# Weight conversion with the sign made by the scaling pass, and another order of the opening

## The chip, the core and the metric

One core of a Trainium2 chip runs the whole program. The metric is the device time of one execution in microseconds: the median of several runs. One execution was also recorded by the hardware profiler; its trace is what the rows below come from.

## What is computed

The inputs q, k and v have 8 batches of 8 heads, 576 positions and 64 columns. The weights are float64 in DRAM, since the random numbers are divided by a float64 square root.

```python
# linear attention: softmax of q over its columns, of k over the positions
kv = einsum('bhsd,bhse->bhde', softmax(k, axis=2), v)
x = einsum('bhsd,bhde->bhse', softmax(q, axis=-1), kv)   # then 4608 x 512
# gated layer, 512 -> 1536 -> 512
g = x @ w_gate;  x = (g * sigmoid(g) * (x @ w_val)) @ w_out
# second layer, 512 -> 1024 -> 512
h = x @ w_in2
solu = h * softmax(h, axis=-1)
out = (solu - mean(solu)) / sqrt(var(solu) + 1e-6) * g_ln @ w_out2
```

## The kernel before

**Blocks.** The 4608 tokens go in nine blocks of 512. For every block the kernel makes the attention's rows x, then for each of 12 slices of 128 columns a gate (wg), a value (wv) and their part of the output (y). The gate's products are followed by a Silu on ScalarE (L979), the value's by a product on VectorE (L984), a cast on ScalarE (L989) and a difference on VectorE (L991). All products of the gated layer keep float32 precision by splitting each operand into an upper part (in the rounded type fp32r) and a rest, and by three matmuls (L945 to L947): upper by upper, upper by rest, rest by upper. The second layer comes after all blocks.

**Weights.** A class Weight (L175) holds one tile of 128 x 1024 float64 words, 1 MB. There are 12 tiles wgv0 to wgv11 (a slice of w_gate and of w_val in each, two DMAs of 512 KB) and six tiles wo0 to wo5 of w_out in the opening, and eight tiles w2r0 to w2r7 of the second layer, one in each later block. A float64 word becomes float32 by moving bits: `scale` (L196) reads the upper 32 bits as a float32 and multiplies them by 2^-112, which moves the exponent to its place; `low_bits` (L204) takes the upper bits of the lower word, by reading one byte of it; and `join` (L227) shifts the upper word left by three and ors the lower one in (L236). The shift drops the sign bit, so it is put into the lower word first: either on VectorE in `join` (L232), or on ScalarE in `sign` (L217 to L225), for the nine tiles in the list SIGNED (L1090). Then `upper` casts to fp32r on ScalarE (L247) and `rest` takes the difference on VectorE (L257).

**Order.** Up to the last block every engine gets its instructions in the order in which the program gives them; nothing reorders them later. The opening (L1074) has named tasks, cut into steps at each yield, and the list ORDER (L27) says which task takes its next step. The names: `lk` loads two heads of keys, `lq` half of the queries, `lv` four heads of values, `lw` and `lo` a weight tile; `kT` turns keys, takes their maximum and exponential; `kB` turns them back; `qm`, `qe`, `qn` are maximum, exponential and normalisation of queries; `pk` multiplies keys with values; `pt` turns queries; `px` makes a quarter of x; `cw` and `co` convert a weight tile in four steps (start on ScalarE, join on VectorE, upper on ScalarE, rest on VectorE); `g`, `v`, `o` are gate, value and output of a slice, with g0, v0, g1 and v1 cut into halves that need two quarters of x each. `s` stores a converted tile to DRAM (store, L269) and `b7`, `b8`, `n2` read tiles 7, 8 and 2 back (L276), since only some stay on the chip; a read-back needs a place that another tile has left, by its products and by its store. `*n` puts n small matmuls on constants on TensorE (keep_warm, L1025 to L1029), to keep it at work; 18 of them lead. `t`, `x`, `m`, `a`, `e`, `kv`, `qm`, `qe`, `qn`, `kvl`, `ql1`, `kvn`, `qnx` prepare the attention of the next block and load for it. All DMAs are issued on SP's queue, one after the other; one that waits holds back those behind it. A later block takes its steps from BLOCK_ORDER (L41).

Of the kernel before, what the change touches and what calls it, by code (L numbers as in the profile page):

```python
# [8 lines left out]
F32 = mybir.dt.float32  # L9
# [3 lines left out]
AF = mybir.ActivationFunctionType  # L13
ALU = mybir.AluOpType
# [4 lines left out]
P = 128  # L19
ENGINES = 'PE', 'DVE', 'Activation', 'Pool'  # L20
U8 = mybir.dt.uint8
F16 = mybir.dt.float16
U16 = mybir.dt.uint16
I16 = mybir.dt.int16
COMPUTE = {getattr(mybir.EngineType, x) for x in ENGINES}

ORDER = """  # L27
lw1 lk01 cw1 *14 kT1 lk00 kT0 kT1 lq0 kT1 kT0 *4 kB11 kB10 kT0 kB11 kB00 kB10 qm0 lk10 kB01 cw1 kB00 kT2 lk11 lq1
kB01 qm0 lw0 kT3 kT2 qm1 cw1 qe0 kT2 kT3 kT3 cw0 qn0 *14 kB31 lv0 qm1 kB21 lo0 kB20 qn0 pt1 kB31 pt0 qe1 cw1 lv1
kB30 qn1 kB21 *6 pk1 kB20 pt0 pt1 kB30 pk1 pk1 pk0 pk0 pk0 *5 px1 qn1 lw3 px0 co0 px1 pt2 lw2 pt2 pt3 cw0 co0 pk2  # L30
px0 pk3 pt3 lw4 cw0 pk2 kvl0 pk2 pk3 *11 px2 co0 pk3 px2 lo1 cw3 px0 cw0 px1 px2 *4 px3 lw5 co0 g0 v0 px3 g1 px3 cw2
g0 v0 g0 cw3 cw2 v0 cw2 v1 lw6 g1 cw2 v0 cw3 v0 g1 v1 cw3 g2 v1 o0 cw4 v1 m0 g2 v1 v2 cw4 co1 a0 cw4 co1 ql1 g3 cw5
v2 co1 v2 g3 cw4 o1 cw6 a0 v3 v2 g4 cw5 v3 v3 lw7 cw5 g4 co1 o2 qm cw6 lo2 cw7 v4 v3 co2 qm cw5 e0 cw6 v4 o3 lo3 co2
g5 v4 co2 v5 qe cw6 lw9 v4 g5 co3 g6 co2 cw7 v5 lw10 o4 s2 lw8 qn s3 co3 v5 v5 kv0 v6 kvl1 g6 cw7 cw7 cw8 kv0 kv0 o5
v6 cw8 kv0 v6 co3 v6 g7 lo4 co3 cw8 cw9 v7 g7 cw8 qn cw9 cw10 v7 o6 g8 t1 v7 cw9 m1 v8 t1 v7 cw9 cw10 a1 o7 co4 g8
g9 v8 v8 t1 lw11 co4 cw10 t0 s7 s8 t0 v9 t0 g9 v8 co4 cw11 x1 x0 v9 s9 v9 cw10 x0 co4 t3 x1 t3 a1 g10 s4 x0 t3 x1 o8
t2 lo5 v9 e1 kv1 g10 o9 cw11 kv1 t2 cw11 t2 kv1 kv1 kvn v10 qnx cw11 x2 b7 s10 x3 v10 co5 v10 s1 s0 g11 x2 v10 x3
co5 s11 co5 x3 x2 co5 g11 v11 b8 n2 v11 v11 v11 o10
""".split()

BLOCK_ORDER = """  # L41
# [50 lines left out]
def attention_glu_solu_kernel(  # L92
# [23 lines left out]
    nc = tc.nc  # L116
# [22 lines left out]
    def f32(ap):  # L139
        return ap.bitcast(F32)  # L140

    const = ctx.enter_context(tc.tile_pool(name="const", bufs=1))
# [9 lines left out]
    nc.gpsimd.memset(neg_half, -0.5)  # L152
    floor_bias = const.tile([P, 1], F32, name="floor_bias")
    nc.gpsimd.memset(floor_bias, -15.5 / 32)
    sign_bias = const.tile([P, 1], F32, name="sign_bias")
    nc.gpsimd.memset(sign_bias, 127.5 * 2.0 ** -10)
    warm = const.tile([P, 1], F32, name="warm")
    nc.scalar.activation(out=warm, in_=floor_bias, func=AF.Exp)
    kv_parts = {}
# [15 lines left out]
    class Weight:  # L175
# [6 lines left out]

        def __init__(self, pool, tag, srcs, name, scales=None):
            self.pool, self.tag, self.name, self.scales = pool, tag, name, scales
            self.w, self.done, self.signed = None, False, False
            self.raw = pool.tile([P, 2 * DM, 2], U32, tag=tag, name=f"{name}r")
            n = 2 // len(srcs)
            for i, src in enumerate(srcs):
                nc.sync.dma_start(
                    out=self.raw[:, i * n * DM:(i + 1) * n * DM, :]  # L190
                    .rearrange("p n w -> p (n w)")
                    .rearrange("p (a m) -> p a m", a=src.shape[1]),
                    in_=src,
                )

        def scale(self, on_pool=False):  # L196

            high = f32(self.raw[:, :, 1])
            if on_pool:
                nc.gpsimd.tensor_scalar(out=high, in0=high, scalar1=2.0 ** -112, scalar2=None, op0=ALU.mult)  # L200
            else:
                nc.scalar.activation(out=high, in_=high, func=AF.Copy, scale=2.0 ** -112)

        def low_bits(self):  # L204

# [8 lines left out]
            self.scale()  # L214
            self.low_bits()

        def sign(self):  # L217

            raw = self.raw.rearrange("p n w -> p (n w)")
            top = raw.bitcast(U8).rearrange("p (n b) -> p n b", b=8)  # L220
            sign = raw.bitcast(I16).rearrange("p (n b) -> p n b", b=4)
            nc.scalar.activation(
                out=sign[:, :, 1], in_=top[:, :, 7], func=AF.Prelu, scale=-2.0 ** -10, bias=sign_bias, alpha=2.0 ** 27
            )
            self.signed = True  # L225

        def join(self, pool, tag, bufs=1):  # L227

            low, high = self.raw[:, :, 0], self.raw[:, :, 1]
            if not self.signed:  # L230
                words = self.raw.rearrange("p n w -> p (n w)").bitcast(U16).rearrange("p (n b) -> p n b", b=4)
                nc.vector.tensor_scalar(  # L232
                    out=words[:, :, 1], in0=words[:, :, 3], scalar1=1 << 15, scalar2=None, op0=ALU.bitwise_and
                )
            t = pool.tile([P, 2 * DM], U32, tag=tag, bufs=bufs, name="t")
            nc.vector.scalar_tensor_tensor(  # L236
                out=t, in0=high, scalar=3, in1=low,
                op0=ALU.logical_shift_left, op1=ALU.bitwise_or,
            )
            self.x = f32(t)  # L240
# [833 lines left out]
    def opening():  # L1074
# [12 lines left out]
        }  # L1087
        pools = dict(a=wpool, b=w_b, x=ph1x)
        temps = [(tmp, "t2"), (tmp, "yt")]
        SIGNED = [('wgv', 1), ('wgv', 2), ('wgv', 5), ('wgv', 6), ('wgv', 9), ('wgv', 10), ('wo', 1), ('wo', 3), ('wo', 5)]  # L1090
        joined = []

        def convert(nm, i):
            w, _ = W[("wg", i) if nm == "wgv" else ("wo", 2 * i)]
            w.start()
            if (nm, i) in SIGNED:
                w.sign()
            yield
            w.join(*temps[len(joined) % 2])
            joined.append(i)  # L1100
            yield
            w.upper()
            yield
            w.rest()
# [72 lines left out]
        for i in range(NF):  # L1177
            add(f"lw{i}", load_w1, pools[homes["wgv", i][0]], homes["wgv", i], "wgv", i)
            add(f"cw{i}", convert, "wgv", i)
            add(f"g{i}", gate, i)  # L1180
            add(f"v{i}", value, i)
            add(f"o{i}", emit_o, 0, i, i == 0, False)
        for i in range(NF // 2):
            add(f"lo{i}", load_w1, pools[homes["wo", i][0]], homes["wo", i], "wo", i)
            add(f"co{i}", convert, "wo", i)
# [126 lines left out]

    late = []
    opening()
    pend.clear()
    for j in range(1, NB - 1):
# [379 lines left out]
    a, b = 2 * last, 2 * last + 1  # L1696
# [43 lines left out]
```

## Time and profile before

| | us |
|---|---|
| median of 3 runs | 1341.49 (1341.44 to 1341.50) |
| the profiled execution | 1340.76 |
| its span, first to last instruction | 1339.0 |
| TensorE busy (PE) | 1326.7, 99% |
| VectorE busy (DVE) | 909.5, 68% |
| ScalarE busy (ACT) | 773.9, 58% |
| GpSimd busy (POOL) | 45.2, 3% |

The engines run beside one another, so the busy times don't add up to the span. A matmul's row shows its latency, and matmuls overlap. The share of the clock is the part of full speed (2.4 GHz) that TensorE was granted. Times in rows count from the start of the span.

### The profile page before, as it was taken

The page shows a single profiled execution, that of the slowest core. Times are in us where ns is not written, and L with a number is a line of the kernel's source. Part 1 is how long each engine was busy: PE and PEld are TensorE (multiplying, and loading weights), DVE is VectorE, ACT ScalarE, POOL GpSimd, SP SyncE. Part 2 cuts the span into 40 slices and gives each one's busy share as a digit, 9 for nine tenths or more (in the row PEclk, how much of TensorE's full clock was granted, in tenths as well). Part 3 has the DMA queues.
Part 4 walks back from the last instruction along what each step waited for, and adds up shares of the span by engine and source line. Part 5 has one row for each costly group of instructions (what it writes and reads, how often), then busy time and mean ns, then how long its engine had stood idle before and what let it go on. Part 6 is the DMA issues. An engine that isn't in the chain of part 4 may idle for free.

```text
span 1339.0 us, 17601 instructions
## 1 busy us (share of the span) xinstructions
PE 1326.7 (99%) x6572; PEld 1095.2 (82%) x6572; DVE 909.5 (68%) x1564; ACT 773.9 (58%) x1109; POOL 45.2 (3%) x172
## 2 busy tenths in 40 slices
PE   8999999999999999999999999999999999999999
PEld 6788788888888888888888888888888888888887
DVE  6898675675675685676675573564288778778774
ACT  7998465455455465465465443442276766766764
POOL 2001100000000000000000000000000000000000
PEclk9999999999999999999999999999999999999999
DMA  9965983573574565465557445374377666676651
GB/s 282 286 226 203 361 208 108 187 230 115 178 229 137 173 219 152 157 208 164 172 197 213 160 173 166 145 262 162 118 193 190 173 188 179 165 202 172 163 142 40
DMA packets 242918, 247.58 MB, mean 185 GB/s; under 512 B 152080, under 2 KB 216592, under 8 KB 231824
## 3 DMA queue, kind: packets, MB, share of 16 engines
q1 hardware_dynamic: 242832, 246.45, 60.8%
q8 instruction: 52, 0.85, 0.3%
q14 instruction: 34, 0.28, 0.1%
HBM read 162.01 MB, written 59.24 MB: 165 GB/s over the span
## 4 chain that ended last, share of the span: by engine, by line
PE 90%; ACT 5%; DVE 2%; issue 1%; DMA 1%; SPq 0%; ACTq 0%; DVEq 0%
PE wg L945 7%; PE y L945 7%; PE y L947 7%; PE wv L945 7%; PE y L946 7%; PE wg L947 7%; PE wg L946 7%; PE wv L947 7%; PE wv L946 7%; PE y L1571 5%; PE y L1569 5%; PE y L1570 5%; PE h L945 4%; PE h L947 4%; PE h L946 4%
## 5 line engine op out<-in xcount | busy, mean ns | idle before, releaser
L984 DVE TENSOR_TENSOR st<-st,wv 128x512 f32<-128x512 f32 x108 | 74.1, 686 | 165.4 <-PE wv L947 153.1
L945 PE MATMUL wg<-xh,wgv 128*128 128x512 f32 x432 | 170.0, 394 | 2.3 <-DMA wgv<-w_dram 2.3
L945 PE MATMUL wv<-xh,wgv 128*128 128x512 f32 x432 | 169.3, 392 | 0.2 <-DVE st L984 0.2
L947 PE MATMUL wg<-xh,wgv 128*128 128x512 f32 x432 | 168.5, 390 | 0.0
L946 PE MATMUL y<-a,wo 128*128 128x512 f32 x432 | 168.2, 389 | 0.2 <-DVE a L991 0.2
L947 PE MATMUL y<-a,wo 128*128 128x512 f32 x432 | 168.2, 389 | 0.1
L946 PE MATMUL wg<-xl,wgv 128*128 128x512 f32 x432 | 168.3, 390 | 0.0
L945 PE MATMUL y<-a,wo 128*128 128x512 f32 x432 | 168.3, 390 | 0.0
L946 PE MATMUL wv<-xl,wgv 128*128 128x512 f32 x432 | 168.2, 389 | 0.0
L947 PE MATMUL wv<-xh,wgv 128*128 128x512 f32 x432 | 168.1, 389 | 0.0
L979 ACT ACTIVATE st<-wg 128x512 f32<-128x512 f32 x108 | 64.7, 599 | 141.7 <-PE wg L947 140.9
L991 DVE TENSOR_TENSOR a<-st,a 128x512 fp32r<-128x512 f32 x108 | 74.4, 688 | 76.2 <-ACT a L989 75.5
L1569 PE MATMUL y<-w,zhl 128*128 128x512 f32 (+1 forms) x296 | 113.6, 384 | 0.0
L1570 PE MATMUL y<-w,zhl 128*128 128x512 f32 (+1 forms) x296 | 113.5, 383 | 0.0
L1571 PE MATMUL y<-w,zhl 128*128 128x512 f32 (+1 forms) x296 | 113.5, 383 | 0.0
L989 ACT CAST a<-st 128x512 fp32r<-128x512 f32 x108 | 67.0, 621 | 73.0 <-DVE st L984 46.6
L945 PEld LDWEIGHTS wg<-xh,wgv 128*128 128x128 f32 x432 | 81.1, 188 | 19.3 <-ACT kt L545 2.7
L947 PEld LDWEIGHTS wg<-xh,wgv 128*128 128x128 f32 x432 | 81.1, 188 | 17.8 <-DVE wgv L257 0.7
L947 PEld LDWEIGHTS y<-a,wo 128*128 128x128 f32 x432 | 81.1, 188 | 17.4 <-DVE wo L257 0.6
L946 PEld LDWEIGHTS y<-a,wo 128*128 128x128 f32 x432 | 81.1, 188 | 17.4 <-DVE a L991 0.5
L945 PEld LDWEIGHTS wv<-xh,wgv 128*128 128x128 f32 x432 | 81.1, 188 | 17.3 <-DVE st L984 0.4
L947 PEld LDWEIGHTS wv<-xh,wgv 128*128 128x128 f32 x432 | 81.1, 188 | 17.1
(289 smaller groups left out, 2542.5 us busy)
## 6 DMA issues: line engine op xcount, KB each, us to landing
wgv<-w_dram SPq DMA_DIRECT2D x64, 1024.0 KB, 6.0
yf_dram<-yf SPq DMA_DIRECT2D x56, 512.0 KB, 3.8
yh<-yf_dram SPq DMA_DIRECT2D x18, 896.0 KB, 5.0
yl<-yf_dram SPq DMA_DIRECT2D x18, 896.0 KB, 7.1
w_dram<-wgv SPq DMA_DIRECT2D x10, 1024.0 KB, 11.0
out_dram<-ot SPq DMA_DIRECT2D x35, 256.0 KB, 2.9
kt<-in_k_dram SPq DMA_DIRECT2D x14, 512.0 KB, 4.6
vt<-in_v_dram SPq DMA_DIRECT2D x56, 128.0 KB, 3.4
```

The lines of the kernel that those rows point to most:

```text
L945: nc.tensor.matmul(out=po, lhsT=wh, rhs=rh, start=start, stop=False, **k)
L946: nc.tensor.matmul(out=po, lhsT=wh, rhs=rl, start=False, stop=False, **k)
L947: nc.tensor.matmul(out=po, lhsT=wl, rhs=rh, start=False, stop=stop, **k)
L979: nc.scalar.activation(out=st, in_=pg, func=AF.Silu)
L984: nc.vector.tensor_tensor(out=st, in0=st, in1=pv, op=ALU.mult)
L989: nc.scalar.copy(out=ah, in_=st)
L991: nc.vector.tensor_tensor(out=al, in0=st, in1=f32(ah), op=ALU.subtract)
L1569: nc.tensor.matmul(out=po[:, s], lhsT=zh[:, c, :], rhs=wh[:, s], start=first, stop=False)
L1570: nc.tensor.matmul(out=po[:, s], lhsT=zh[:, c, :], rhs=wl[:, s], start=False, stop=False)
L1571: nc.tensor.matmul(out=po[:, s], lhsT=zl[:, c, :], rhs=wh[:, s], start=False, stop=last)
```

## The change

The sign pass on ScalarE, its list, its constant and the VectorE sign operation are gone. The scaling pass is now a Prelu, an activation that multiplies negative results by a slope: 2^32 in this case. It raises the exponent of a negative word by 32, which is the bit that the shift by three moves into the sign's place. An unused variant of scale on POOL is removed. ORDER is another list: 48 small matmuls in place of 76, and other places for loads, conversions, stores and read-backs.

```diff
 ORDER = """
-lw1 lk01 cw1 *14 kT1 lk00 kT0 kT1 lq0 kT1 kT0 *4 kB11 kB10 kT0 kB11 kB00 kB10 qm0 lk10 kB01 cw1 kB00 kT2 lk11 lq1
-kB01 qm0 lw0 kT3 kT2 qm1 cw1 qe0 kT2 kT3 kT3 cw0 qn0 *14 kB31 lv0 qm1 kB21 lo0 kB20 qn0 pt1 kB31 pt0 qe1 cw1 lv1
-kB30 qn1 kB21 *6 pk1 kB20 pt0 pt1 kB30 pk1 pk1 pk0 pk0 pk0 *5 px1 qn1 lw3 px0 co0 px1 pt2 lw2 pt2 pt3 cw0 co0 pk2
-px0 pk3 pt3 lw4 cw0 pk2 kvl0 pk2 pk3 *11 px2 co0 pk3 px2 lo1 cw3 px0 cw0 px1 px2 *4 px3 lw5 co0 g0 v0 px3 g1 px3 cw2
-g0 v0 g0 cw3 cw2 v0 cw2 v1 lw6 g1 cw2 v0 cw3 v0 g1 v1 cw3 g2 v1 o0 cw4 v1 m0 g2 v1 v2 cw4 co1 a0 cw4 co1 ql1 g3 cw5
...
-g9 v8 v8 t1 lw11 co4 cw10 t0 s7 s8 t0 v9 t0 g9 v8 co4 cw11 x1 x0 v9 s9 v9 cw10 x0 co4 t3 x1 t3 a1 g10 s4 x0 t3 x1 o8
-t2 lo5 v9 e1 kv1 g10 o9 cw11 kv1 t2 cw11 t2 kv1 kv1 kvn v10 qnx cw11 x2 b7 s10 x3 v10 co5 v10 s1 s0 g11 x2 v10 x3
-co5 s11 co5 x3 x2 co5 g11 v11 b8 n2 v11 v11 v11 o10
+lk00 lk01 kT0 kT0 lq0 kT1 kT0 kT1 qm0 *4 kB01 lw0 kT1 kB01 lk11 kB00 kB11 lk10 kB10 qm0 *9 kT3 kB00 cw0 cw0 qe0 kT2
+kT3 lq1 kT2 kB10 qm1 kT3 *9 kB31 qm1 qn0 kB11 kB30 kT2 kB31 kB30 lv0 kB21 *3 pk0 cw0 lw1 qn0 kB21 qe1 pk0 pk1 pk1
+qn1 pk0 pt0 kB20 pt1 pk1 pt0 lv1 pt1 qn1 *5 px0 kB20 px1 pt3 pk3 cw1 lw2 cw0 pk3 pt3 lo0 px0 pk2 pk2 px0 pk3 pk2 pt2
+px3 pt2 px1 px2 cw1 cw1 px1 g0 v0 cw1 g1 px2 px2 px3 cw2 px3 co0 lw3 kvl0 g0 v0 v1 g0 lw4 cw2 co0 cw2 v0 g1 v1 lo1
+v0 co0 cw2 v0 lw5 co0 g1 cw3 v1 g2 o0 cw3 v1 v2 m0 cw3 v1 cw4 cw3 g2 cw4 a0 co1 cw4 co1 v2 g3 cw4 lw6 cw5 v2 g3 ql1
...
+cw10 g9 v8 a1 v8 t1 g9 cw10 s2 x0 x1 co4 a1 t2 v8 s4 x1 cw10 x0 lw11 x0 v9 s1 x1 e1 lo5 v9 o8 cw10 kv1 t2 cw11 kvn
+t2 v9 s10 kv1 v9 g10 kv1 t3 cw11 kv1 o9 g10 t3 cw11 t3 v10 x2 s0 cw11 co5 v10 s11 qnx v10 co5 v10 co5 x3 x3 x2 co5
+g11 x3 v11 x2 n2 g11 o10 v11 s9 b8 v11 b7 v11
 """.split()
...
-        def scale(self, on_pool=False):
+        def scale(self):
 
             high = f32(self.raw[:, :, 1])
-            if on_pool:
-                nc.gpsimd.tensor_scalar(out=high, in0=high, scalar1=2.0 ** -112, scalar2=None, op0=ALU.mult)
-            else:
-                nc.scalar.activation(out=high, in_=high, func=AF.Copy, scale=2.0 ** -112)
+            nc.scalar.activation(out=high, in_=high, func=AF.Prelu, scale=2.0 ** -112, alpha=2.0 ** 32)
...
-        def sign(self):
-
-            raw = self.raw.rearrange("p n w -> p (n w)")
-            top = raw.bitcast(U8).rearrange("p (n b) -> p n b", b=8)
-            sign = raw.bitcast(I16).rearrange("p (n b) -> p n b", b=4)
-            nc.scalar.activation(
-                out=sign[:, :, 1], in_=top[:, :, 7], func=AF.Prelu, scale=-2.0 ** -10, bias=sign_bias, alpha=2.0 ** 27
-            )
-            self.signed = True
-
         def join(self, pool, tag, bufs=1):
 
             low, high = self.raw[:, :, 0], self.raw[:, :, 1]
-            if not self.signed:
-                words = self.raw.rearrange("p n w -> p (n w)").bitcast(U16).rearrange("p (n b) -> p n b", b=4)
-                nc.vector.tensor_scalar(
-                    out=words[:, :, 1], in0=words[:, :, 3], scalar1=1 << 15, scalar2=None, op0=ALU.bitwise_and
-                )
...
-        SIGNED = [('wgv', 1), ('wgv', 2), ('wgv', 5), ('wgv', 6), ('wgv', 9), ('wgv', 10), ('wo', 1), ('wo', 3), ('wo', 5)]
...
-            if (nm, i) in SIGNED:
-                w.sign()
```

## Rows read from the trace of the kernel before

**Rows 1.** The page: span, and busy time of each engine, share, instructions.

```profile
span 1339.0 us, 17601 instructions
PE 1326.7 (99%) x6572; PEld 1095.2 (82%) x6572; DVE 909.5 (68%) x1564; ACT 773.9 (58%) x1109; POOL 45.2 (3%) x172
```

**Rows 2.** Windows: length, busy us of each engine, TensorE clock, DMA share, GB/s.

```profile
0.00:20.00 20.00, 15.85 (x167) 12.34 (x167) 9.31 (x12) 14.25 (x17) 8.50 (x30) 1.00 0.99 261
20.00:40.00 20.00, 18.68 (x169) 13.85 (x170) 15.99 (x25) 18.01 (x30) 0.60 (x5) 0.91 1.09 285
...
36.00:60.00 24.00, 24.00 (x107) 19.69 (x106) 20.07 (x32) 23.87 (x23) 0.00 (x0) 1.00 1.10 250
60.00:100.00 40.00, 39.87 (x209) 32.51 (x208) 36.68 (x43) 39.73 (x40) 0.60 (x5) 1.00 0.76 255
100.00:120.00 20.00, 19.54 (x94) 15.54 (x94) 17.52 (x31) 16.47 (x20) 0.00 (x0) 1.00 0.72 281
...
140.00:160.00 20.00, 17.70 (x79) 14.37 (x78) 13.92 (x29) 8.26 (x11) 0.00 (x0) 1.00 0.95 364
160.00:440.00 280.00, 280.00 (x1452) 231.84 (x1451) 183.88 (x340) 149.19 (x235) 4.20 (x34) 1.00 0.58 178
```

The engines of a window stand in the order PE, PEld, DVE, ACT, POOL.

**Rows 3.** TensorE's waits from 0 to 260 us: total, times, longest.

```profile
PE wg L945 <- DMA wgv<-w_dram: 2.3, 1, 2.3
```

**Rows 4.** TensorE's timeline: start, duration, line, operation, tiles; first product, twelve of a later gate.

```profile
35.16 0.80 PE L945 MATMUL wg<-xh,wgv 128*128 128x512 f32 x1
...
151.96 0.39 PE L947 MATMUL wg<-xh,wgv 128*128 128x512 f32 x1
...
154.68 0.39 PE L947 MATMUL wv<-xh,wgv 128*128 128x512 f32 x1
```

**Rows 5.** ScalarE's timeline up to the first product, weight passes.

```profile
6.06 1.14 ACT L202 ACTIVATE wgv1r<-wgv1r 128x1024 f32<-128x1024 f32 x1 [3.84 <-DMA wgv1r<-in_moe_w_val_dram]
...
8.44 2.58 ACT L222 ACTIVATE wgv1r<-wgv1r,sign_bias 128x1024 int16<-128x1024 uint8 x1
...
26.45 1.17 ACT L202 ACTIVATE wo0r<-wo0r 128x1024 f32<-128x1024 f32 x1
27.53 1.26 ACT L207 ACTIVATE wo0r<-wo0r,floor_bias 128x1024 uint32<-128x1024 uint8 x1
...
32.85 1.05 ACT L247 CAST wo<-t 128x1024 fp32r<-128x1024 f32 x1
```

**Rows 6.** Groups by line and form: count, busy us, mean ns, idle before.

```profile
L979 ACT ACT_TABLE_LOAD x22 | 28.2, 1283 | 20.5 <-PE wg L947 20.2
...
L222 ACT ACTIVATE wgv5r<-wgv5r,sign_bias 128x1024 int16<-128x1024 uint8 x1 | 2.7, 2678 | 0.0
...
L222 ACT ACTIVATE wgv1r<-wgv1r,sign_bias 128x1024 int16<-128x1024 uint8 x1 | 2.6, 2577 | 0.1
...
L1529 ACT COPY zt<-wT 128x1024 uint16<-128x1024 uint16 x34 | 46.5, 1367 | 17.9 <-DMA wT<-w 17.6
...
L232 DVE TENSOR_SCALAR w2r0r<-w2r0r 128x1024 uint16<-128x1024 uint16 x1 | 1.3, 1337 | 0.0
```

**Rows 7.** DMA issues from 0 to 60 us: count, KB each, us to landing.

```profile
heads<-in_k_dram SPq DMA_DIRECT2D x4, 288.0 KB, 6.8
vt<-in_v_dram SPq DMA_DIRECT2D x8, 144.0 KB, 6.3
raw<-in_q_dram SPq DMA_DIRECT2D x2, 512.0 KB, 8.0
...
wgv1r<-in_moe_w_gate_dram SPq DMA_DIRECT2D x1, 512.0 KB, 3.6
```

**Rows 8.** SP's timeline at the end of the opening: start, time to the end.

```profile
133.13 0.53 SPq L276 DMA_DIRECT2D wgv<-w_dram  x1
133.71 2.32 SPq L269 DMA_DIRECT2D w_dram<-wgv  x4
145.68 7.61 SPq L276 DMA_DIRECT2D wgv<-w_dram  x2
```

More of the change, by code (lines that the diff above doesn't have):

```diff
@@ L23 @@
 U16 = mybir.dt.uint16
-I16 = mybir.dt.int16
 COMPUTE = {getattr(mybir.EngineType, x) for x in ENGINES}
 ORDER = """
-lw1 lk01 cw1 *14 kT1 lk00 kT0 kT1 lq0 kT1 kT0 *4 kB11 kB10 kT0 kB11 kB00 kB10 qm0 lk10 kB01 cw1 kB00 kT2 lk11 lq1
-kB01 qm0 lw0 kT3 kT2 qm1 cw1 qe0 kT2 kT3 kT3 cw0 qn0 *14 kB31 lv0 qm1 kB21 lo0 kB20 qn0 pt1 kB31 pt0 qe1 cw1 lv1
-kB30 qn1 kB21 *6 pk1 kB20 pt0 pt1 kB30 pk1 pk1 pk0 pk0 pk0 *5 px1 qn1 lw3 px0 co0 px1 pt2 lw2 pt2 pt3 cw0 co0 pk2
-px0 pk3 pt3 lw4 cw0 pk2 kvl0 pk2 pk3 *11 px2 co0 pk3 px2 lo1 cw3 px0 cw0 px1 px2 *4 px3 lw5 co0 g0 v0 px3 g1 px3 cw2
@@ L32 @@
-g0 v0 g0 cw3 cw2 v0 cw2 v1 lw6 g1 cw2 v0 cw3 v0 g1 v1 cw3 g2 v1 o0 cw4 v1 m0 g2 v1 v2 cw4 co1 a0 cw4 co1 ql1 g3 cw5
-v2 co1 v2 g3 cw4 o1 cw6 a0 v3 v2 g4 cw5 v3 v3 lw7 cw5 g4 co1 o2 qm cw6 lo2 cw7 v4 v3 co2 qm cw5 e0 cw6 v4 o3 lo3 co2
-g5 v4 co2 v5 qe cw6 lw9 v4 g5 co3 g6 co2 cw7 v5 lw10 o4 s2 lw8 qn s3 co3 v5 v5 kv0 v6 kvl1 g6 cw7 cw7 cw8 kv0 kv0 o5
-v6 cw8 kv0 v6 co3 v6 g7 lo4 co3 cw8 cw9 v7 g7 cw8 qn cw9 cw10 v7 o6 g8 t1 v7 cw9 m1 v8 t1 v7 cw9 cw10 a1 o7 co4 g8
-g9 v8 v8 t1 lw11 co4 cw10 t0 s7 s8 t0 v9 t0 g9 v8 co4 cw11 x1 x0 v9 s9 v9 cw10 x0 co4 t3 x1 t3 a1 g10 s4 x0 t3 x1 o8
@@ new lines @@
+px3 pt2 px1 px2 cw1 cw1 px1 g0 v0 cw1 g1 px2 px2 px3 cw2 px3 co0 lw3 kvl0 g0 v0 v1 g0 lw4 cw2 co0 cw2 v0 g1 v1 lo1
+v0 co0 cw2 v0 lw5 co0 g1 cw3 v1 g2 o0 cw3 v1 v2 m0 cw3 v1 cw4 cw3 g2 cw4 a0 co1 cw4 co1 v2 g3 cw4 lw6 cw5 v2 g3 ql1
+co1 cw6 v2 cw5 co1 o1 v3 v3 cw6 g4 o2 cw5 lw7 v3 v3 lo2 v4 cw5 cw6 g5 qm g4 cw7 v4 o3 cw6 qm s3 lw8 a0 lo3 v4 lw9
+co2 v4 co2 g5 qe v5 e0 co2 v5 cw7 g6 kv0 lw10 v5 co2 cw7 lo4 g6 qn o4 kv0 cw8 v5 cw7 v6 cw8 o5 kv0 kv0 cw9 kvl1 co3
+qn v6 co3 v6 cw8 g7 t0 g7 s7 co3 v6 cw8 cw9 v7 s8 co3 co4 co4 t1 g8 cw9 o6 v7 t0 t0 v7 co4 v7 t1 cw9 v8 g8 m1 o7
@@ L154, in attention_glu_solu_kernel @@
     nc.gpsimd.memset(floor_bias, -15.5 / 32)
-    sign_bias = const.tile([P, 1], F32, name="sign_bias")
-    nc.gpsimd.memset(sign_bias, 127.5 * 2.0 ** -10)
     warm = const.tile([P, 1], F32, name="warm")
@@ L184, in __init__ @@
             self.pool, self.tag, self.name, self.scales = pool, tag, name, scales
-            self.w, self.done, self.signed = None, False, False
+            self.w, self.done = None, False
             self.raw = pool.tile([P, 2 * DM, 2], U32, tag=tag, name=f"{name}r")
```

## The prediction

> **What bounds the kernel now.** I first read the page's busy times: TensorE is busy for 1326.7 of 1339.0 us [rows 1], so only its missing 12.3 us can be had, and the question is where they lie. The windows answer it [rows 2]. TensorE lacks 4.15 us in the first 20 us and 1.32 in the next 20, nothing from 36 to 60, 0.13 from 60 to 100, 0.46 from 100 to 120, 2.3 from 140 to 160, nothing from 160 to 440. In the opening, "busy" also flatters: much of that work is transposes and filler matmuls that keep the clock up. The number to watch is the start of the first product wg, at 35.16 us [rows 4]. From there to 440 us TensorE lacks only those 2.9 us. The wait list names the largest one: a product wg waits 2.3 us for a weight read back from DRAM [rows 3].
>
> What delays the first product? ScalarE works from 6.06 us on [rows 5] and is busy 18.01 us of 20 to 40, 23.87 of the 24 from 36 to 60 and 39.73 of the 40 after them [rows 2]. VectorE has gaps there (36.68 of 40). The DMA share is about 1 until 60 us. So the opening is paced by ScalarE, with the loads close behind. This is the stage in which a pass less on ScalarE can move TensorE; from 160 us on it can't, since TensorE has no idle time to give back there (what is missing after 440 us lies beyond the weights' conversion).
>
> **The change, part by part.**
>
> The sign passes. Nine tiles lose a ScalarE pass that takes between 2.58 and 2.68 us (first and last of nine rows) [rows 6]: 9 x 2.63 = 23.7 us of ScalarE. The other nine tiles of the opening and the eight of the last weights lose a VectorE pass of 1.34 us [rows 6], 17 x 1.34 = 22.8 us. The eight lie under a TensorE that never stops, and the nine beside a ScalarE that is the later engine: I count all of VectorE's part at nothing. If ScalarE's cover goes, VectorE is the next engine, and it only has less to do. POOL loses one memset; it idles most of the opening [rows 2], nothing.
>
> The scaling pass, 18 + 8 of them, becomes an activation with a slope. No row shows it on full words. Lower bound: the pass that it replaces, same tile, same operands, in place, 1.14 us [rows 5]. Upper bound: the sign pass, the same function, up to 2.68 us [rows 6]. They differ in operands too: the sign pass reads single bytes and writes two-byte halves eight bytes apart. Byte reads are not what costs, since the low-bits pass reads the same bytes and takes 1.26 us [rows 5]. Two-byte writes into every second half take a plain copy 1.37 us [rows 6], against 1.05 us for the cast with full-word writes [rows 5]; so part of the excess has such a source. I take 1.15 us, by the nearest row in operands, and keep 2.68 for the range. At 1.15 ScalarE gains 23.7 us; at 2.68 it gets 18 x 1.53 = 27.5 us against 23.7, a loss of 3.8. A lower price than the copy's is excluded, because the pass touches the same words. No table load comes in: the loads stand where the function changes, most of them at the Silu line [rows 6], and no row has one at the sign pass, which runs before the first Silu and after it.
>
> The Trainium skill, "ScalarE: Activation LUTs", section "What ACT_TABLE_LOAD costs", has every function at one rate per element, 186 ns + 0.833 ns an element with immediates: an estimate of 1.04 us here, near my lower bound. Read as a price of the function, the sign rows speak against it; no row here separates function from operands.
>
> The opening's order up to the first product. Before, tile wgv1 is loaded and converted first, and wo0 ahead of the first product. After, the two first key loads lead, wgv0 comes fourth, wgv1 is converted late, and the three ScalarE passes of wo0 go behind the first halves of g0, v0 and g1. From ScalarE's queue ahead of the first product go: the sign of wgv1, 2.58; wo0's scale and low bits, 1.17 + 1.26; its upper half, 1.05 [rows 5]. Sum 6.06 us. On SP the two loads of wgv1 move behind all keys, queries and the first values, the one of wo0 behind the second values and wgv2, on VectorE wo0's join and rest behind the first products. Against it, ScalarE starts later: its first work is now an exponential of keys, not a weight. The first 512 KB landed 3.6 us after their issue [rows 7], so 576 KB of keys land near 5 us, and transposes and a maximum on VectorE follow: near 7 us in place of 6.06, 1.0 us lost. The start moves from 35.16 to 35.16 - 6.06 + 1.0 = 30.1 us, 5.1 us earlier.
>
> Are the loads ready? All keys, queries and values of the first batch and two weight tiles are 4 x 288 + 2 x 512 + 8 x 144 + 4 x 512 = 5376 KB, 5.5 MB [rows 7]; before, the 1 MB of wo0 was also queued ahead of the last values on SP. At 270 GB/s, between the 261 and 285 of the first two windows [rows 2], that is 20.4 us; with about 2 us before the first data move, 22.4. The last values then need a product, VectorE, ScalarE, a second product and its two parts, some 5 us by my estimate: 28 us. So the loads come 2 us ahead of ScalarE, and this is the lower end.
>
> TensorE's fillers fall from 76 to 48. All are ahead of the first product, in idle time: nothing. The cover is the chain of ScalarE and VectorE; if it goes, a filler less is a gain.
>
> Behind the first product ScalarE has wgv2 and wo0 to start, 2.4 us each, a table load, 1.28 [rows 6], an upper half, 1.05, and four passes over half as many columns, each under that: at most 11.3 us. TensorE has two gates and two values in the meantime, 48 products at 0.227 us (twelve take 2.72 from start to start [rows 4]), 10.9 us. It just fits, and further on ScalarE has 21 us less in a stretch that it filled: the 0.13 and 0.46 us from 60 to 120 go. I take 0.6.
>
> The end of the opening. The load that TensorE waited 2.3 us for is tile 2, issued in the second of the two read-backs that start at 145.68 us [rows 8]. On SP it stood behind one read-back and four stores, and its room comes free when the store of tile 11 is done. The new order puts the read-back of tile 7 and the stores of tiles 1 and 9 elsewhere and tile 8's behind it: 2 MB less in front, at 364 GB/s [rows 2] 5.5 us. It needs 2.3. I count 2.3 gained. What is queued behind the moved read-backs (tile 3 and later ones) is wanted a product or more later: nothing.
>
> **Sum.** 5.1 + 0.6 + 2.3 = 8.0 us. The profiled execution took 1340.76 us (span 1339.0); 1332.8. The median of the runs is 0.73 above it: **1333.5 us**.
>
> **The rivals.**
>
> Slower: the slope costs. If the function itself takes 2.68 us, ScalarE gets 3.8 us more over the opening, which it paces; the order's shifts only move its queue, and the end moves with its total: 1341.5 + 3.8 = 1345.3. The point from which ScalarE's total grows is 1.15 + 23.7/18 = 2.47 us. For it: the sign rows are the only ones of this function. Against: byte and half-word operands. 9 in 100.
>
> Nothing on the path: both engines get lighter, but the new order has as much standing in front of the products, or a new wait on SP replaces the old; the conversions get cheaper without TensorE starting earlier. 1341.0. For it: ScalarE's chain has waits, whose places I carried over. 12 in 100.
>
> Loads: with the keys first and the weights later, wgv2, wo0 and wgv3 land as they are wanted. The start comes at 33 (2.2 gained), the read-back is gained (2.3), and a new wait of 1 us stands at g2: 1338.0. For it: a DMA share of 1 until 60 us [rows 2]. Against: of these loads ScalarE waits for none now, but for 3.84 us at the very start [rows 5]. 12 in 100.
>
> The clock. It is 0.91 over 20 to 40 us [rows 2], after a window in which TensorE was idle for 4.15 us: 1.8 us lost to the low level, and TensorE is on no critical chain there. With 28 fillers fewer it can be at 1.2 GHz when the products begin; a spell like that costs the same 1.8 us, two 3.6: 1335.3 to 1337.1. 7 in 100. The Trainium skill, "TensorE: Matmul & The Clock Gate", section "Part 1: The HAM clock gate", has the clock follow how busy TensorE was just before, which speaks against thinning fillers; by it the sum would be this rival's.
>
> **How the numbers follow.** My forecast gets 60 in 100. Two thousandths, 0.2% or 2.7 us, are about what a measurement of this kernel can tell from no change. Faster: forecast, loads and clock, 0.79. Same: nothing on the path, 0.12. Slower: 0.09. The range goes from 1329.5 (the start at 28, and another 2 us of waits that I can't see) to 1341.0 (nothing on the path); the slope at its upper bound is left out.
>
> **What would show it.** Right: the scaling rows near 1.15 us and no sign rows; the first wg near 30 us; ScalarE under 90% from 36 to 100; no wait for the read-back near 150. Wrong: scaling rows above 2 us; the first wg after 33; a wait of wg or y on VectorE or a load before 60 us; a granted clock of a half after the first wg.

## The result, and the profile after

The changed kernel takes 1330.34 us (median of four runs, 1329.15 to 1330.58), the kernel before 1341.47: a ratio of 0.9919, interval 0.9902 to 0.9936. That is 11.1 us faster where 8.0 were forecast; it lies in the range, near its lower end. Its profiled execution took 1330.36 us, span 1328.6; against the profiled execution of before that is 10.4 us.

The windows of the changed kernel, to be read beside [rows 2] (length, busy us of PE, PEld, DVE, ACT and POOL, granted clock, DMA share, GB/s):

```profile
0.00:20.00 20.00, 15.51 (x162) 11.81 (x164) 8.47 (x10) 11.18 (x18) 7.52 (x29) 1.00 0.96 239
20.00:40.00 20.00, 19.47 (x169) 14.59 (x170) 15.08 (x25) 18.79 (x30) 0.60 (x5) 1.00 0.98 282
36.00:60.00 24.00, 24.00 (x108) 19.87 (x107) 21.64 (x34) 22.52 (x26) 0.00 (x0) 1.00 0.93 282
60.00:100.00 40.00, 40.00 (x215) 32.99 (x214) 35.70 (x45) 34.70 (x40) 0.60 (x5) 1.00 0.86 319
100.00:120.00 20.00, 20.00 (x132) 16.72 (x131) 15.81 (x34) 12.11 (x18) 3.18 (x13) 1.00 0.51 177
...
140.00:160.00 20.00, 20.00 (x94) 16.33 (x94) 13.14 (x17) 10.12 (x15) 0.00 (x0) 1.00 0.96 349
```

ScalarE falls from 39.73 to 34.70 us of the 40 between 60 and 100. VectorE hardly falls, from 36.68 to 35.70, although its sign passes are gone: the products come closer together, so it has as much to do in the same time. From 36 to 60 us ScalarE is still busy for 94% of the time, from 60 to 100 for 87%, together for 89%: only just under the 90% that the prediction named as a sign. TensorE has no idle time left from 36 to 440 us (the windows left out, 120 to 140 and 160 to 440, are full), and the clock stays at its upper level over 20 to 40, where it was 0.91.

TensorE's timeline, the first product of the gated layer, the answer to the first of [rows 4]:

```profile
30.27 0.80 PE L924 MATMUL wg<-xh,wgv 128*128 128x512 f32 x1
```

TensorE's waits from 0 to 260 us, all of them (total, times, longest). They all lie ahead of that product; the wait of [rows 3] is not among them:

```profile
PE kT L477 <- DMA heads<-in_k_dram: 1.5, 1, 1.5
PE y L540 <- POOL vt L404: 1.1, 1, 1.1
PE y L1008 <- PEq L1701: 0.8, 1, 0.8
PE y L503 <- ACT kx L489: 0.7, 1, 0.7
PE px L790 <- ACT qx L693: 0.3, 1, 0.3
```

ScalarE's timeline, its first work and the weight passes, beside [rows 5]:

```profile
7.65 0.74 ACT L489 ACTIVATE kx<-kT,nk 128x576 f32<-128x576 f32 x1 [5.42 <-DVE nk L484]
...
11.81 1.10 ACT L196 ACTIVATE wgv0r<-wgv0r 128x1024 f32<-128x1024 f32 x1 [1.70 <-DMA wgv0r<-in_moe_w_val_dram]
...
24.62 1.18 ACT L196 ACTIVATE wgv1r<-wgv1r 128x1024 f32<-128x1024 f32 x1
25.69 1.24 ACT L201 ACTIVATE wgv1r<-wgv1r,floor_bias 128x1024 uint32<-128x1024 uint8 x1
...
34.23 1.15 ACT L196 ACTIVATE wo0r<-wo0r 128x1024 f32<-128x1024 f32 x1
```

The pass with the slope takes 1.10 to 1.18 us, as the plain one did. The first work comes at 7.65 us, and wo0 stands behind the first product.

SP's timeline at the end of the opening, beside [rows 8]:

```profile
122.23 1.99 SPq L248 DMA_DIRECT2D w_dram<-wgv  x3
...
132.71 0.35 SPq L255 DMA_DIRECT2D wgv<-w_dram  x1
...
133.63 9.38 SPq L255 DMA_DIRECT2D wgv<-w_dram  x2
```

The last stores but one start 11.5 us earlier than before (122.23 against 133.71), and tile 2 is read back from 132.71 us on, wanted at 148.84.

Where the 10.4 us between the two profiled executions lie, counted from start to start of TensorE's matmuls: 4.9 us are the earlier first product (35.16 to 30.27). 2.5 us are the wait for tile 2. 1.55 us are short stalls between 40 and 140 us: spacings that exceed 0.227 us by over 0.06 sum to 2.13 us before and to 0.58 after, those that end at a matmul of the attention left out. 0.9 us lie in the second layer, where a product waited 0.7 us on VectorE, which itself had waited for a DMA transpose; that one moves from run to run (below, the filler run). The rest, 0.5 us, is spread in smaller pieces.

### The profile page after: what moved, and what is told of

The parts are those of the page before. It is cut to its first block, busy times and chain, and to the rows that moved or that the text cites. A ratio compares the mean times of both kernels' runs of the same rounds, so it can differ in the third digit from the quotient of the medians.

```text
span 1328.6 us, 17522 instructions
## 1 busy us (share of the span) xinstructions
PE 1320.3 (99%) x6544; PEld 1092.0 (82%) x6544; DVE 886.3 (67%) x1547; ACT 750.8 (57%) x1100; POOL 44.8 (3%) x171
## 4 chain that ended last, share of the span: by engine, by line
PE 98%; DMA 1%; DVE 0%; ACT 0%; issue 0%; SPq 0%; ACTq 0%
PE wg L924 8%; PE wv L924 7%; PE wg L925 7%; PE wg L926 7%; PE y L924 7%; PE wv L925 7%; PE wv L926 7%; PE y L926 7%; PE y L925 7%; PE y L1546 5%; PE y L1547 5%; PE y L1545 5%; PE h L924 4%; PE h L925 4%; PE h L926 4%; PE pk L540 1%
```

## The experiments

**The new conversion under the old order.**

```diff
 (the changed kernel)
-ORDER = the new list
+ORDER = the list of the kernel before
```

> The changed conversion (scaling with a slope, no sign passes) under the old order. Queue theory (the gain is what leaves ScalarE's queue ahead of the first product, what it no longer holds up until 126 us, and the read-back of tile 2 moved forward): the sign of wgv1, 2.58 us, leaves the queue ahead of the first product, which starts near 32.6 in place of 35.16; the short waits between 60 and 126 us, some 1.9 us in all, go; the wait of 2.3 us for tile 2 stays. Near 1337. Rival 1, the order alone brings the gain: 1341.5. Rival 2, the passes alone bring it: 1330.3.

Measured: 1334.84 us, ratio 0.995 (0.9935 to 0.9964), 6.6 us faster than before; between the rivals, and 2 us better than the queue theory had it. The first product starts at 34.02 us, 1.1 us earlier than before and not 2.58. The sign of wgv1 is out of ScalarE's queue, but the two exponentials of keys behind it now wait for VectorE's maxima of keys that land at 7.46 us. ScalarE's timeline:

```profile
9.64 0.74 ACT L489 ACTIVATE kx<-kT,nk 128x576 f32<-128x576 f32 x1 [1.77 <-DVE nk L484]
10.77 0.74 ACT L489 ACTIVATE kx<-kT,nk 128x576 f32<-128x576 f32 x1 [0.39 <-DVE nk L484]
```

The second ends at 11.51 us, where it ended at 12.11 before, and `kv_first`, further down the chain, begins at 24.50 us, not 25.09. So of 2.58 us taken out of the queue 0.6 arrive: where a queue is relieved ahead of a load, the load takes up the slack. The other 0.5 us are not ScalarE's. Before, two sign passes on VectorE stand ahead of a small step, `rs`, that `kv_first` on ScalarE needs. VectorE's timeline before, without a gap, and then in this kernel, where the same step waits for TensorE instead:

```profile
26.74 1.33 DVE L232 TENSOR_SCALAR wgv0r<-wgv0r 128x1024 uint16<-128x1024 uint16 x1
...
29.25 1.32 DVE L232 TENSOR_SCALAR wo0r<-wo0r 128x1024 uint16<-128x1024 uint16 x1
...
31.75 0.15 DVE L567 TENSOR_SCALAR rs<-y 128x1 f32<-128x1 f32 x1
```

```profile
30.28 0.16 DVE L546 TENSOR_SCALAR rs<-y 128x1 f32<-128x1 f32 x1 [0.59 <-PE y L540]
```

Before, ScalarE stood idle for 0.39 us and began that `kv_first` at 32.19 us; here it begins at 31.05. The stalls after 40 us go nearly as in the changed kernel, and the wait for tile 2 shrinks to 1.2 us (TensorE's waits):

```profile
PE wg L924 <- DMA wgv<-w_dram: 1.2, 1, 1.2
```

**The old conversion under the new order.**

```diff
 (the kernel before)
-ORDER = the list of the kernel before
+ORDER = the new list
```

> The old conversion with its sign passes under the new order. Queue theory: wgv1's sign pass stands in ScalarE's queue again, the first product starts near 33 in place of 30.3; ScalarE is full until 100 us and products wait 1 to 3 us for converted tiles; the read-back of tile 2 is still early. Near 1335. Rival 1, the order alone brings the gain: 1330.3. Rival 2, the passes alone: 1341.5.

Measured: 1349.87 us, ratio 1.006 (1.0043 to 1.0077): 8.4 us slower than before, worse than any of the three. The first product starts at 35.54 us, and then products wait for weights. TensorE's waits up to 260 us, the three of them on converted weights:

```profile
PE y L947 <- DVE wo L257: 3.2, 2, 2.4
PE wg L947 <- DVE wgv L257: 2.9, 4, 1.1
...
PE y L945 <- ACT wo L247: 1.4, 1, 1.4
```

The new list converts tiles just before they are wanted. With the sign passes in between they come late. The order by itself is worth less than nothing: it pays only with the shorter conversion.

**All signs on VectorE, under the new order.**

```diff
 (the kernel before, with the new list)
-        SIGNED = [('wgv', 1), ('wgv', 2), ('wgv', 5), ('wgv', 6), ('wgv', 9), ('wgv', 10), ('wo', 1), ('wo', 3), ('wo', 5)]
+        SIGNED = []
```

> The old conversion under the new order with no sign pass on ScalarE: all 26 are made by the VectorE pass of 1.34 us. ScalarE then has the same passes as in the changed kernel. If the gain under the new order is ScalarE's (VectorE's passes cost nothing, as the prediction had it), the time is near that of the changed kernel, 1330.3 to 1332. If VectorE is on the way from a weight's landing to its product too, each tile comes 1.34 us later, products wait for tiles, and it lies between 1333 and the 1349.9 of the run with nine sign passes on ScalarE.

Measured: 1344.26 us, ratio 1.0017 (1.0007 to 1.0027); 14 us above the changed kernel, whose passes on ScalarE it shares. Its windows:

```profile
36.00:60.00 24.00, 22.94 (x101) 18.50 (x100) 21.98 (x34) 20.29 (x22) 0.00 (x0) 1.00 1.03 250
60.00:100.00 40.00, 35.50 (x180) 28.23 (x179) 39.48 (x45) 29.55 (x34) 0.60 (x5) 0.96 0.75 255
```

VectorE is busy 39.48 us of 40, ScalarE 29.55 and TensorE 35.50: here VectorE is the bound. Its longest effects on TensorE, from the waits:

```profile
PE y L947 <- DVE wo L257: 3.7, 3, 2.0
...
PE wg L947 <- DVE wgv L257: 2.4, 2, 1.3
```

The first product starts at 32.28 us, 2.0 later than in the changed kernel: wgv0 lands 0.65 us later in this execution, and its sign pass of 1.34 us stands in VectorE's queue on the way. So the VectorE passes do cost: 18 of them in the opening, 24.1 us of VectorE, take 14 us here. Both engines had to be relieved.

**wo0 put back ahead of the first product.**

```diff
-px3 pt2 px1 px2 cw1 cw1 px1 g0 v0 cw1 g1 px2 px2 px3 cw2 px3 co0 lw3 ...
+px3 pt2 co0 px1 px2 cw1 cw1 px1 g0 v0 cw1 g1 px2 px2 px3 cw2 px3 lw3 ...
```

> The changed kernel, with the first two ScalarE passes of tile wo0 put back ahead of the first product (before the second upper part of x). Queue theory: 2.4 us more in ScalarE's queue, so the first product starts near 32.6 and the end is 2 to 2.4 us later, near 1332.5. Rival: the start hangs on the loads of the last values or on VectorE; ScalarE has the room, and nothing changes, 1330.3.

Measured: 1334.27 us, ratio 0.9944 (0.9928 to 0.996), 3.9 us later than the changed kernel by the medians. The first product starts at 32.09 us, and then stands again. ScalarE's timeline first, then TensorE's:

```profile
31.54 1.14 ACT L196 ACTIVATE wo0r<-wo0r 128x1024 f32<-128x1024 f32 x1
32.58 1.19 ACT L201 ACTIVATE wo0r<-wo0r,floor_bias 128x1024 uint32<-128x1024 uint8 x1
33.66 0.58 ACT L801 CAST xh<-px 128x512 fp32r<-128x512 f32 x1
```

```profile
34.30 0.49 PE L924 MATMUL wg<-xh,wgv 128*128 128x512 f32 x1 [0.95 <-ACT xh L801]
35.02 0.50 PE L925 MATMUL wg<-xl,wgv 128*128 128x512 f32 x1 [0.23 <-DVE xl L803]
```

The product waits for the upper part of x, which now stands behind wo0 in ScalarE's queue; from start to start the stall costs 1.7 us. So ScalarE has no room for wo0 there, and in this the queue theory is right and the rival wrong. The later start is not wo0's: the work before the product at 32.09 us was through ScalarE when wo0 came, at 31.54. This execution had its keys 0.8 us later (TensorE waited 2.3 us for them, not 1.5) and a clock of 0.83 over the first 20 us, and began 1.8 us later. The two together are the 3.55 us between the profiled executions; the one of the four runs with a mean clock of 1.0 took 1332.04 us, 1.7 us over the changed kernel.

**Tile 2 read back last.**

```diff
-g11 x3 v11 x2 n2 g11 o10 v11 s9 b8 v11 b7 v11
+g11 x3 v11 x2 s9 b8 b7 n2 g11 o10 v11 v11 v11
```

> The changed kernel, with the store of tile 9 and the read-backs of tiles 8 and 7 put ahead of the read-back of tile 2 on SP. Queue theory: tile 2 is issued 10 us later, near 143, lands near 149, and the third gate of the second block, which wants it near 149, waits 0 to 2.5 us: 1330.3 to 1333. Rival: the wait went because the stores are spread, not because of the place in the queue: no wait, 1330.3.

Measured: 1330.92 us, ratio 0.992 (0.9905 to 0.9935), the same as the changed kernel. SP's timeline, where tile 2 is the third of the last row and issued at 142.2:

```profile
124.18 1.99 SPq L248 DMA_DIRECT2D w_dram<-wgv  x3
...
131.37 11.22 SPq L255 DMA_DIRECT2D wgv<-w_dram  x3
```

It lands at 149.24 us, and its gate runs at 150.25 without a wait. So the place of the read-back in the queue is not what removed the wait; the rival is right. The stores in front of it start at 124 us here and at 122 in the changed kernel; before, they started at 133.71, the read-back could go only when the store of tile 11 was done, and that was at 152.97.

**The memset of the values first.**

```diff
-... kT3 *9 kB31 qm1 qn0 kB11 kB30 kT2 kB31 kB30 lv0 kB21 *3 pk0 ...
+... kT3 *9 kB31 lv0 qm1 qn0 kB11 kB30 kT2 kB31 kB30 kB21 *3 pk0 ...
```

> The changed kernel, with the load of the first values named ahead of the second subtraction on POOL, so that its memset no longer waits behind that subtraction; SP's queue stays as it is. Theory: the 1.15 us for which TensorE's first product of keys and values waits for POOL goes, ScalarE's wait of 0.99 us at 21.85 us goes with it, and the first product of the gated layer starts near 29.3: 1329.3. Rival: the wait only moves, to the values' own landing or into ScalarE's queue: 1330.3.

Measured: 1330.11 us, ratio 0.9922 (0.9907 to 0.9937): no difference that can be told. The wait for POOL is gone, and another stands in its place (TensorE's waits); the first product starts at 29.86 us:

```profile
PE pq L686 <- DVE qt L671: 0.7, 1, 0.7
```

**Without the fillers.**

```diff
-lk00 lk01 kT0 kT0 lq0 kT1 kT0 kT1 qm0 *4 kB01 lw0 kT1 kB01 lk11 kB00 kB11 lk10 kB10 qm0 *9 kT3 kB00 cw0 cw0 qe0 kT2
+lk00 lk01 kT0 kT0 lq0 kT1 kT0 kT1 qm0 kB01 lw0 kT1 kB01 lk11 kB00 kB11 lk10 kB10 qm0 kT3 kB00 cw0 cw0 qe0 kT2
...
```

> The changed kernel without the 30 fillers behind the leading 18. Clock theory: TensorE is idle more before the first product, its clock is at the lower level in parts of the opening and perhaps when the products begin: 1.8 to 3.6 us later, 1332 to 1334. Queue theory: TensorE is not on the chain there, the clock is back before the first product: 1330.3, a few tenths either way.

Measured: 1335.14 us, ratio 0.9956 (0.9939 to 0.9972), 4.8 us above the changed kernel: the clock theory. It is more than the 1.8 to 3.6 us that it said, but the start alone is 3.5 us later in the trace, which it did say. The windows of this kernel (the clock is the third number from the end):

```profile
10.00:13.00 3.00, 0.36 (x3) 0.11 (x1) 0.00 (x0) 0.92 (x2) 1.75 (x1) 1.00 1.10 230
...
14.00:20.00 6.00, 5.81 (x55) 4.75 (x51) 4.34 (x5) 4.47 (x9) 0.43 (x1) 0.50 1.12 220
20.00:27.00 7.00, 5.46 (x61) 5.24 (x61) 5.75 (x12) 4.10 (x8) 2.22 (x8) 0.50 1.20 269
...
28.00:33.00 5.00, 4.60 (x60) 2.72 (x59) 3.19 (x7) 4.90 (x10) 0.00 (x0) 1.00 1.05 392
```

and two of the same windows in the changed kernel:

```profile
14.00:20.00 6.00, 4.03 (x49) 2.90 (x47) 5.83 (x7) 5.28 (x11) 2.05 (x3) 1.00 1.16 233
20.00:27.00 7.00, 6.71 (x100) 5.07 (x102) 5.81 (x11) 5.92 (x11) 0.60 (x5) 1.00 1.14 275
```

Without fillers TensorE is nearly idle from 10 to 13 us, while it waits for keys, and is then granted half of its clock, 1.2 GHz, from 14 to 27 us, past the point where it has work again. Turning keys (4.11 us in place of 2.20) and making the first products of keys and values (2.87 in place of 1.62) then take nearly twice as long, and the product behind them starts at 33.73 us. The keys landed 0.6 us later in this execution than in the changed kernel's, but that isn't what holds the clock down: in the run with tile 2 last they landed later still, at 13.97 us and not 13.41, and with fillers the time at half clock was some 3.4 us there and not 13. All four runs without fillers have a mean clock of 0.994 to 0.996, those of the changed kernel 0.999 to 1.0. Another 1.8 us of the 5.1 between the two profiled executions is no effect of the fillers: a stall at 997 us, where VectorE waited 2.48 us for a transposing DMA to land (1.34 in the profiled execution of before, 0.80 in that of after).

**The sign pass with another function.**

```diff
-                out=sign[:, :, 1], in_=top[:, :, 7], func=AF.Prelu, scale=-2.0 ** -10, bias=sign_bias, alpha=2.0 ** 27
+                out=sign[:, :, 1], in_=top[:, :, 7], func=AF.Identity, scale=-2.0 ** -10, bias=sign_bias
```

> The kernel before, with the sign pass on ScalarE as an Identity on the same operands in place of a Prelu; it leaves out the slope, so the signs of nine tiles are not made. If the two-byte writes into every fourth place are what costs, its rows stay at 2.6 us and the time at 1341.5; if the function costs, they fall to 1.2 to 1.4 us and the kernel gains some of the 11 us.

Measured: 1341.32 us in the one run. First and last of its nine rows, by line and form (busy us, mean ns):

```profile
L222 ACT ACTIVATE wo1r<-wo1r,sign_bias 128x1024 int16<-128x1024 uint8 x1 | 2.7, 2672 | 0.0
...
L222 ACT ACTIVATE wgv1r<-wgv1r,sign_bias 128x1024 int16<-128x1024 uint8 x1 | 2.6, 2580 | 0.1
```

Not the function, the operands: with Identity the pass takes as long as it did with the slope.

**The changed kernel again, and with memset first and 24 fillers.** The first is unedited, the second:

```diff
-lk00 lk01 kT0 kT0 lq0 kT1 kT0 kT1 qm0 *4 kB01 lw0 kT1 kB01 lk11 kB00 kB11 lk10 kB10 qm0 *9 kT3 kB00 cw0 cw0 qe0 kT2
-kT3 lq1 kT2 kB10 qm1 kT3 *9 kB31 qm1 qn0 kB11 kB30 kT2 kB31 kB30 lv0 kB21 *3 pk0 ...
+lk00 lk01 kT0 kT0 lq0 kT1 kT0 kT1 qm0 *4 kB01 lw0 kT1 kB01 lk11 kB00 kB11 lk10 kB10 qm0 *24 kT3 kB00 cw0 cw0 qe0 kT2
+kT3 lq1 kT2 kB10 qm1 kT3 *9 kB31 lv0 qm1 qn0 kB11 kB30 kT2 kB31 kB30 kB21 *3 pk0 ...
```

> The changed kernel again, unedited, to be compared with the next two on one chip: 1330.3, and how far its start moves from run to run with the landing of the second pair of key loads (TensorE waited for them 1.5 us at 12.85 us in its first trace, and 1.5 to 3.3 us in the other kernels that share its opening).

> The changed kernel with the values' load named ahead of the second subtraction on POOL (as in the memset run) and 24 fillers in place of 9 ahead of the wait for the second pair of key loads. Clock theory: the spell of 3.4 us at half clock near 14 us, which the memset run had, goes, and with the memset's 1.1 us the first product starts 1 to 2 us earlier than in the unedited kernel of this call: 0.1% faster. Rival: the start hangs on the landing of the loads and on ScalarE's queue, the same within 0.3 us; or the 15 fillers, 1.6 us, push the turning of the keys back where the loads come early, and it is 0.5 us slower.

Measured on one chip: 1330.08 us (ratio 0.9913, 0.9898 to 0.9928) and 1329.86 us (0.9911, 0.9895 to 0.9927). The same; the rival holds. In the edited kernel TensorE waits for neither the keys nor POOL to speak of, and its first product still starts at 30.06 us, because the transposes of queries wait for VectorE (TensorE's waits):

```profile
PE pq L686 <- DVE qt L671: 1.2, 1, 1.2
...
PE kT L477 <- DMA heads<-in_k_dram: 0.3, 1, 0.3
```

What VectorE in turn waits for is the first weight. The chain that leads to the first product, followed back in each trace, comes to the landing of wgv0 in the changed kernel, in its second execution and in the edited one (start, duration):

```profile
2.72 9.01 DMA wgv0r<-in_moe_w_val_dram
```

```profile
2.72 8.21 DMA wgv0r<-in_moe_w_val_dram
```

```profile
2.71 8.83 DMA wgv0r<-in_moe_w_val_dram
```

It lands at 11.73, 10.93 and 11.54 us, and the first products start at 30.27, 29.47 and 30.06: 18.5 us later in all three.

No version here beats the changed kernel.

## Why the prediction held, point by point

**The price of the slope** was right: 1.10 to 1.18 us, taken at 1.15 (the lower bound of 1.14 was no bound: the plain pass itself takes 1.11 to 1.20), and the upper bound of 2.68 falls with the Identity run. The excess of the sign pass comes with its operands; that it is their two-byte writes is argued from the low-bits pass [rows 5], which reads single bytes in 1.26 us. The Trainium skill, "ScalarE: Activation LUTs", section "What ACT_TABLE_LOAD costs", has one rate for every function; the trace agrees for the function, and the 2.6 us rows show that operands can double the time all the same.

**The start**, 5.1 us earlier by the sum, came 4.9 us earlier, and that it came so near is in part luck, since the path is not the one of the sum. Its terms fared as follows. The sign of wgv1 gave 0.6 of its 2.58 us under the old order, because the keys' landing takes up the rest. wo0, put back, stalls the product for 1.7 us, where its first two passes were put at 2.43. ScalarE's first work came at 7.65 us, 1.6 us later and not 1.0. And "the loads come 2 us ahead of ScalarE" failed: under the new order the first product stands 18.5 us behind the landing of wgv0 in three executions, and in the changed kernel, from the join of wgv0 at 14.10 us VectorE, not ScalarE, is busy without a gap to 26.0. What the sum left out is that the new order asks for wgv0 sooner: SP issues it at 2.17 us, not 4.96, and ScalarE begins it at 11.81 us, not 18.07. Nor does the sum count the spell at half clock from 20 to 24 us, which is gone. How much of the 4.9 us each of these is worth no run here separates.

**Short stalls** were mis-sized: 0.6 forecast, 1.55 measured. I read them from TensorE's idle time, and a matmul's row of 0.39 us covers the first 0.16 us of every stall. The stall at 106.20 us had 0.23 us of idle in its row and 0.70 us from start to start.

**Tile 2**: 2.3 forecast, the wait is gone. But "2 MB less in front" in SP's queue was not the reason, since with 3 MB put back in front there is no wait either. (By the two lists it is 3 MB, the read-backs of tiles 7 and 8 and the store of tile 1; the store of tile 9 went ahead of that group.) The stores start 11.5 us earlier, as TensorE reaches the products of keys and values that SP's loads wait for at 116 us, not 126.

**VectorE's part at nothing** failed. "The nine beside a ScalarE that is the later engine" misses some 0.5 us in the kernel before, where ScalarE waits behind the sign passes of wgv0 and wo0, and it doesn't hold for a kernel that has taken ScalarE's passes away and wants its weights sooner: with VectorE's passes kept, 14 us. The forecast didn't suffer, since the change removes both. But it was right by a sum whose parts are not independent: passes alone 6.6 us, order alone -8.4, both 11.1.

**The fillers at nothing** was wrong as a rule, though not for the 48 of this change. "The cover is the chain of ScalarE and VectorE; if it goes, a filler less is a gain" missed that TensorE's transposes are on that chain and take twice as long at the lower clock. The rival's mechanism is real, and in the run without fillers the start is later by 3.5 us, with 13 us at half clock; the rival had 1.8 to 3.6. In the kernel before, too, the chain runs through TensorE from 20.03 to 24.62 us, where it is granted 0.55 and 0.59 of its clock (20 to 22 and 22 to 24 us), so "on no critical chain there" was wrong. The Trainium skill, "TensorE: Matmul & The Clock Gate", section "Part 1: The HAM clock gate", ties the clock to how busy TensorE was before; the two sets of windows agree.

The remaining 0.9 us of the profiled difference, in the second layer, was not forecast and is no effect of the change as far as these runs show: it follows the landing of a DMA.

## What to carry to other kernels

A forecast that comes out can still have the wrong path: follow the chain back to the landing it begins with before you credit a shorter queue. A pass removed from the fuller of two engines makes the other the bound as soon as the work moves closer together, so cost the second engine with the work at its new pace, and not in the old trace's gaps. An order written out by hand belongs to the durations that it was searched with: neither half of such a change may be judged alone. Measure TensorE's stalls from start to start of its matmuls, and look for its short work on the chain (transposes, small products) before calling a filler free.

## What the runs showed that I had not expected

The same opening starts its first product at 29.47, 30.27 and 31.67 us in three executions (the changed kernel twice, and the run with tile 2 last, which is edited only behind 120 us). TensorE's wait for the second pair of key loads is 1.2, 1.5 and 3.3 us in them, and wgv0, between the two pairs on SP, lands at 10.93, 11.73 and 12.58 us. So some 2 us of the time hang on when loads land in the first 13 us; edits worth less than that, as the memset, can't be told by these medians.

A ScalarE pass that reads single bytes and writes two-byte results eight bytes apart takes 2.6 us for 1024 columns with either of two functions, against 1.24 us for one that reads the same way and writes full words at the same distance, and 1.15 us for full words in and out. Whether it is the width of the result or its integer type no run here separates.
